# A gated linear attention and a rational feed-forward on one Trainium2 core: v loaded in fp32 and cast on chip into zero-padded heads

## The chip, the cores and the metric

The kernel runs on one core of one Trainium2 chip. The metric is the device time of one execution in microseconds (us). Three timed runs of the kernel before gave 215.76, 216.56 and 216.99 us; the median is 216.56 us.

## What is computed

Two stages follow one another. The first is a linear attention with a gate per key channel, for 4 batches and 8 heads over 768 time steps with heads 48 wide:

```python
f = 1.0 / (1.0 + np.exp(-f_logit))
for t in range(S):
    state = f[:, :, t, :, None] * state + np.einsum('bhd,bhe->bhde', k[:, :, t], v[:, :, t])
    y[:, :, t] = np.einsum('bhd,bhde->bhe', q[:, :, t], state)
```

The 8 heads of y are laid side by side to x, 3072 rows of 384. The second stage multiplies x by `w_in` (384 x 2048), puts every element through a rational function and multiplies by `w_out` (2048 x 384):

```python
h = x @ w_in
P = a[0] + a[1]*h + a[2]*h**2 + a[3]*h**3
Q = 1.0 + abs(b[0])*abs(h) + abs(b[1])*h**2
out = (P / (Q + 1e-06)) @ w_out
```

## The kernel before

The work is cut into 12 units of 256 time steps of one batch: unit n holds batch n mod 4 and stretch n div 4 of the time axis. Within a unit, two blocks of 128 steps are computed in chunked form. Partitions hold pairs of time steps, so a loaded tile of q, k, v or the gate has the form partition, head, i (the step of the pair), channel.

**The order of the work** is written out by hand in a table, `ORDER` (lines 19 to 98). Each entry is the name of a step with a unit number, sometimes a range of head pairs or column blocks, a PSUM slot (`@2`) and a mark (`>ls.1`: begin behind that step). The table is run from first to last, and each engine and each DMA queue takes its instructions in that order; between engines semaphores see to the dependencies. The steps that matter here:

- `ld n f|k|q` (line 193) loads the gate logits, keys or queries of a unit in fp32 on SP's queue. `ld n v` loads v on POOL's (GpSimd's) queue, and that DMA casts it from fp32 to bf16 on the way.
- `ef`, `ls` (lines 271, 276) on ScalarE (ACT) make the logarithm of the gate, `cs` (286) sums it along time on TensorE (PE), `A` (302) takes exponentials on ACT, `xa` (308) multiplies q or k by them on VectorE (DVE), `T` and `Te` (320, 330/332) transpose the results.
- `sc` (345) forms the scores of a block on PE, and `mk` (353) multiplies them by the causal mask while it moves them from PSUM to SBUF, on DVE.
- `kv` (414) multiplies keys by v into the new state on PE, `ae` (441) and `st` (445) apply the decay. `yi` and `yb` (367) form y: `yi` from the old state, `yb` from the masked scores and v. `ye` (435/436) moves y out.
- `yb` writes y transposed, in pieces of 32 channels. Two heads have 96 channels and so three pieces; the middle one takes the last 16 channels of the even head and the first 16 of the odd one. For it, v has to lie as 32 columns with zeros in the other half: `vm n 0` and `vm n 1` (line 360) copy the 16 columns of the even and of the odd heads into a tile `vmp` whose middle 16 columns were set to zero once (line 235). These copies run on POOL.
- `wi` and `wo` (199, 205) load `w_in` and `w_out` in four parts each, on POOL's queue, with a cast to bf16. `h` (454) and `ha`, `hb` (478) are the products with `w_in`; `hy`, `ab`, `sq`, `p1`, `p2`, `pm`, `ln`, `lz`, `ex`, `gm` are the steps of the rational function on DVE and ACT; `zd` and `ta` (519, 549) add two tiles with an accumulating DMA on POOL's queue; `o` (567) is the product with `w_out`, `so` (580) the store.

A loaded tile has three buffers (line 139), also v's. `vmp`, the padded q and k and the states are allocated once, in two copies that units use in turn.

In the table, v's load for unit 0 stands first on POOL's queue, then `vm 0 1`, then the first part of `w_in` (`wi 8 12`), then the second (`wi 12 16 >ls.1`), which begins behind unit 1's logarithm.

## Time and profile before

| what | value |
|---|---|
| median of the timed runs | 216.56 us (215.76 to 216.99) |
| span of the profiled execution, first to last instruction | 214.4 us |
| median of the runs less that span | 2.2 us |
| instructions | 7128 |
| granted TensorE clock, mean | 1.000 |
| POOL busy | 83.7 us |
| moved by DMA | 43.20 MB, of these 25.17 MB read from HBM |
| DMA packets under 512 bytes | 51184 of 61199 |

The profile was taken of one execution. Its own time lies around the span: what precedes the first instruction and follows the last one isn't in the span, and the median of the timed runs is 2.2 us above it. Rows of the timeline give the start, the duration, the engine, the line, the operation, what is written and read, and in square brackets the idle time of the engine just before and what ended it. POOL's time as a queue (its DMA instructions) and as an engine (its copies) stand in the same rows. A DMA row of the issues gives the time from issue to landing.

### The profile page before, as it was taken

The numbers are of one execution on the slowest core, as the hardware profiler recorded it, in microseconds if no ns is written. First come the engines' busy times: TensorE is split into PE (matmuls) and PEld (weight loads), VectorE is DVE, ScalarE is ACT, GpSimd is POOL, SyncE is SP. The second block draws the span as 40 slices with busy tenths as digits, with TensorE's granted clock in tenths as the row PEclk, the third lists the DMA queues.
The fourth block names the chain that finished last, engine by engine and source line by source line (L and its number), as shares of the span: only waits on it lengthen the run. The fifth ranks groups of instructions, "written<-read, shape, count | busy, mean of one in ns | idle before, by whom it ended". The sixth has DMA issues, their size and how long they took to land.

```text
span 214.4 us, 7128 instructions
## 1 busy us (share of the span) xinstructions
PE 201.0 (94%) x3166; PEld 139.9 (65%) x3166; DVE 201.7 (94%) x213; ACT 195.8 (91%) x204; POOL 83.7 (39%) x93
## 2 busy tenths in 40 slices
...
GB/s 143 240 257 217 201 242 197 195 223 223 187 200 248 247 235 219 253 228 203 192 292 193 81 294 215 209 225 208 89 192 200 164 196 126 174 282 151 187 84 148
DMA packets 61199, 43.20 MB, mean 202 GB/s; under 512 B 51184, under 2 KB 55024, under 8 KB 61168
## 3 DMA queue, kind: packets, MB, share of 16 engines
...
q8 instruction: 25, 0.41, 0.8%
q10 hardware_dynamic: 288, 0.20, 0.3%
...
HBM read 25.17 MB, written 4.72 MB: 139 GB/s over the span
## 4 chain that ended last, share of the span: by engine, by line
PE 39%; DVE 29%; ACT 14%; DMA 9%; issue 6%; SPq 2%; POOL 1%; DVEq 0%
PE hp L454 13%; PE op L567 12%; DVE gall L557 6%; DMA w_in_sb<-in_moe_w_in_dram 6%; DVE gall L545 4%; ACT qi L527 4%; ACT hy L484 4%; DVE z L497 3%; DVE h L489 3%; DVE scm L353 3%; DMA fn<-in_f_logit_dram 3%; PE u L505 3%; DVE gall L531 3%; PE y L367 2%; DVE hy L536 2%
## 5 line engine op out<-in xcount | busy, mean ns | idle before, releaser
L567 PE MATMUL op<-w_out_sb,gall 128*128 128x384 bf16 x384 | 69.2, 326 | 0.4 <-DVE gall L557 0.4
L454 PE MATMUL hp<-xT,w_in_sb 128*128 128x256 bf16 x564 | 66.7, 273 | 2.1 <-DMA w_in_sb<-in_moe_w_in_dram 2.0
L454 PEld LDWEIGHTS <-w_in_sb 128*128 128x128 bf16 x564 | 54.2, 98 | 11.5 <-DMA w_in_sb<-in_moe_w_in_dram 2.5
L567 PEld LDWEIGHTS <-gall 128*128 128x128 bf16 x384 | 36.1, 98 | 23.6 <-DVE gall L557 0.8
L484 ACT CAST hy<-hp 128x1024 bf16<-128x1024 f32 x47 | 48.1, 1076 | 2.3 <-PE hp L478 1.4
L527 ACT ACTIVATE qi<-lq 128x2048 bf16<-128x2048 f32 (+1 forms) x26 | 48.0, 1861 | 0.1
L360 POOL COPY vmp<-vn 128x128 bf16<-128x128 bf16 x24 | 35.2, 1516 | 28.4 <-DMA vn<-in_v_dram 22.7
L549 POOL DMA_DIRECT2D gall<-hy x20 | 20.0, 1068 | 53.9 <-ACT lsp L276 10.6
L523 ACT ACTIVATE lq<-z 128x2048 f32<-128x2048 bf16 (+1 forms) x20 | 36.8, 1874 | 0.0
L353 DVE TENSOR_TENSOR scm<-sc,mask 128x1024 bf16<-128x1024 f32 x24 | 29.0, 1215 | 1.9 <-PE sc L345 1.7
L489 DVE TENSOR_TENSOR h<-hy 128x4096 bf16<-128x4096 bf16 (+2 forms) x19 | 28.5, 1500 | 0.0
L557 DVE TENSOR_TENSOR gall<-gall,qi 128x4096 bf16<-128x4096 bf16 (+2 forms) x17 | 28.2, 1666 | 0.2
L545 DVE TENSOR_TENSOR gall<-gall,h 128x4096 bf16<-128x4096 bf16 (+2 forms) x17 | 28.1, 1652 | 0.0
L519 POOL DMA_DIRECT2D z<-h x17 | 19.3, 1366 | 17.0 <-PE u L505 6.0
L302 ACT ACTIVATE A<-cs 128x768 f32<-128x768 f32 (+1 forms) x26 | 19.4, 799 | 1.8 <-PE cs L286 1.8
L193 POOL DMA_DIRECT2D vn<-in_v_dram x12 | 12.4, 1030 | 15.7 <-PE y L367 7.9
L531 DVE TENSOR_SCALAR gall<-hy,a_sb 128x4096 bf16<-128x4096 bf16 (+1 forms) x14 | 16.9, 1208 | 0.0
L536 DVE TENSOR_SCALAR hy<-hy,a_sb 128x4096 bf16<-128x4096 bf16 (+1 forms) x14 | 16.6, 1185 | 0.0
L497 DVE TENSOR_SCALAR z<-hy 128x4096 uint16<-128x4096 uint16 (+2 forms) x19 | 15.7, 834 | 0.4 <-ACT hy L484 0.4
L330 ACT COPY qkT<-tp 128x1024 f32<-128x1024 f32 x11 | 11.6, 1058 | 3.2 <-PE tp L320 3.2
L320 PE MATMUL tp<-ident,qkp 128*128 128x128 bf16 x192 | 12.9, 219 | 0.8 <-DVE qkp L308 0.5
L320 PEld LDWEIGHTS <-qkp 128*128 128x128 bf16 x192 | 11.5, 98 | 2.5 <-DVE qkp L308 0.9
...
## 6 DMA issues: line engine op xcount, KB each, us to landing
...
fn<-in_f_logit_dram SPq DMA_DIRECT2D x11, 384.0 KB, 8.5
kn<-in_k_dram SPq DMA_DIRECT2D x11, 384.0 KB, 12.1
qn<-in_q_dram SPq DMA_DIRECT2D x11, 384.0 KB, 11.3
out_dram<-osb SPq DMA_DIRECT2D x11, 384.0 KB, 5.1
...
w_in_sb<-in_moe_w_in_dram POOLq DMA_DIRECT2D x4, 384.0 KB, 10.1
```

Source lines behind the costliest of these rows:

```text
L320: nc.tensor.transpose(t[:, x, i, p, :], s["qk"][:, i, x, 2 * p:2 * p + 2, :].rearrange("t h d -> t (h d)"), ident)
L353: return nc.vector.tensor_mul(t, s["sc", g].rearrange("s r a i t -> s (r a) (i t)"), mb)
L360: nc.gpsimd.tensor_copy(s["vm"][:, :, :, 32 * x:32 * x + 16], src)
L454: nc.tensor.matmul(t[:, m - m0, :], w_in_sb[:, kk, m * P:(m + 1) * P], s["x"][:, kk].rearrange("p i j t -> p (i j t)"), start=(kk == 0), s ...
L484: (nc.scalar.copy if eng == "s" else nc.vector.tensor_copy)(fl(big(s, "hy", "hy", 3), m0, m1), fl(s["hp", m0], 0, m1 - m0))
L489: return nc.vector.tensor_mul(fl(big(s, "h2", "h2", 2), m0, m1), fl(s["hy"], m0, m1), fl(s["hy"], m0, m1))
L523: nc.scalar.activation(fl(lq, m0, m1), fl(s["z"], m0, m1), AF.Ln, scale=regs[2], bias=1.0 + 1e-6)
L527: nc.scalar.activation(fl(qi, m0, m1), fl(lq, m0, m1), AF.Exp, scale=-1.0)
L531: return nc.vector.tensor_scalar(fl(big(s, "g", "gall", 3), m0, m1), fl(s["hy"], m0, m1), a_sb[:, 3:4], a_sb[:, 2:3], op0=ALU.mult, op1=AL ...
L545: return nc.vector.tensor_mul(fl(s["g"], m0, m1), fl(s["g"], m0, m1), fl(s["h2"], m0, m1))
L557: return nc.vector.tensor_mul(fl(s["g"], m0, m1), fl(s["g"], m0, m1), fl(qi, m0, m1))
L567: nc.tensor.matmul(s["op", j][:, j, 0:DM], s["g"][:, m, P * j:P * j + P], w_out_sb[:, m, :], start=(s["on", j] == 1), stop=(s["on", j] == KF))
```

## The change

v is now loaded like q and k: in fp32, on SP's queue, into a tile `vn` with one buffer. A new step `vc n par` (line 360 again) casts the four even heads (`par` 0) or the four odd heads (`par` 1) to bf16 into a new tile `vpd`, which has for each head 64 columns: an even head in columns 0 to 47, an odd head in columns 16 to 63, the other 16 set to zero once. So the three pieces of 32 columns of a head pair can be read from `vpd` as they stand; `vm`, `vmp` and the reads of `vn` by `yb` and `kv` are gone. The casts run on POOL, except those of unit 0: `vc 0 0 s` runs on ACT and `vc 0 1 v` on DVE. Each unit's load of v stands right behind the second cast of the unit before. Eighteen of the 22 casts on POOL have a mark (`>pm.2.0.16`) that holds them until a DVE step is done; in most cases the step that follows on DVE is an `mk`. The mask is stored in bf16.

```diff
-    mask = consts.tile([P, 2, 2, R], F32, name="mask")
+    mask = consts.tile([P, 2, 2, R], BF16, name="mask")
-    vmp = [consts.tile([P, 2, HP, 48], BF16, name=f"vmp{i}") for i in range(2)]
+    vpd = [consts.tile([P, HP, 2, 2, E], BF16, name=f"vpd{i}") for i in range(2)]
 def load(n, what, *args):
-        eng = nc.gpsimd if what == "v" else nc.sync
-            s[what] = ld.tile([P, H, 2, D], BF16 if what == "v" else F32, name=what + "n")
+            s[what] = ld.tile([P, H, 2, D], F32, name=what + "n", bufs=1 if what == "v" else 3)
-        i = eng.dma_start(...)
+        i = nc.sync.dma_start(...)
 def const_z(i):
-            nc.vector.memset(vmp[i][:, :, :, 16:32], 0.0)
+            nc.vector.memset(vpd[i][:, :, 0, :, D:E], 0.0)
+            nc.vector.memset(vpd[i][:, :, 1, :, 0:E - D], 0.0)
-    def vm(n, x):
-        s = unit(n)
-        vv = s["v"].rearrange("p (a r) i d -> p r i a d", r=2)
-        src = vv[:, 0, :, :, 32:48] if x == 0 else vv[:, 1, :, :, 0:16]
-        nc.gpsimd.tensor_copy(s["vm"][:, :, :, 32 * x:32 * x + 16], src)
+    def vc(n, par, *args):
+        s = unit(n)
+        hold = [x[1:] for x in args if x.startswith(">")]
+        copy = nc.scalar.copy if "s" in args else (nc.vector if "v" in args else nc.gpsimd).tensor_copy
+        i = copy(s["vp"][:, :, par, :, 16 * par:16 * par + D],
+                 s["v"].rearrange("p (a r) i d -> p r a i d", r=2)[:, par])
+        if hold:
+            behind(i, hold[0])
+        return i
 def yb(n, a0=0, a1=HP, sl=None):
-                        if kk == 1:
-                            w = s["vm"][r, i0, a, 16 * par:16 * par + 32]
-                        else:
-                            w = s["v"][r, 2 * a + par, i0, 16 * par:16 * par + 32]
+                        e = 32 * (kk - par)
+                        w = s["vp"][r, a, par, i0, e:e + 32]
 def kv(n, sl=None):
-                                         s["qk"][r, i, 1, 2 * a + par, :], s["v"][r, 2 * a + par, i, :],
+                                         s["qk"][r, i, 1, 2 * a + par, :], s["vp"][r, a, par, i, 16 * par:16 * par + D],
 ORDER, two places
-ld 0 q 0 2; ld 1 f; ld 0 v; ab_ a s; ...
-xa 0 1 0 2; T 0 2 4 @0; vm 0 1; kv 0 @3; Te 0 2 4; wi 8 12; ...
+ld 0 q 0 2; ld 0 v; ld 1 f; ab_ a s; ...
+xa 0 1 0 2; T 0 2 4 @0; vc 0 0 s; vc 0 1 v; ld 1 v; kv 0 @3; Te 0 2 4; wi 8 12; ...
```

The order on the engines at three places follows, the kernel before first and the change second. On POOL at the start of the program, behind the constants, before (`vn_158`, `vn_355` and `vn_445` are v of units 0, 1 and 2):

```order
L193 DMA vn_158<-in_v_dram 128x8x96
L360 COPY vmp0_94<-vn_158 128x8x16 [waits DMASW0_49]
L199 DMA w_in_sb_110<-in_moe_w_in_dram 128x3x512
L199 DMA w_in_sb_110<-in_moe_w_in_dram 128x3x512 [waits Activation_49]
L360 COPY vmp0_94<-vn_158 128x8x16
L193 DMA vn_355<-in_v_dram 128x8x96
L199 DMA w_in_sb_110<-in_moe_w_in_dram 128x3x512 x2
L193 DMA vn_445<-in_v_dram 128x8x96
```

And with the change (`vn_220`, `vn_541`, `vn_846` are v of units 1, 2 and 3):

```order
L199 DMA w_in_sb_110<-in_moe_w_in_dram 128x3x512
L199 DMA w_in_sb_110<-in_moe_w_in_dram 128x3x512 [waits Activation_49]
L199 DMA w_in_sb_110<-in_moe_w_in_dram 128x3x512 x2
L360 CAST vpd1_95<-vn_220 128x4x2x48 [waits DMAHW4_49,DVE_49]
L360 CAST vpd1_95<-vn_220 128x4x2x48 [waits DVE_49]
L550 DMA gall_673<-hy_467 128x2048 [waits DVE_49,Activation_49]
L205 DMA w_out_sb_111<-in_moe_w_out_dram 128x4x384
L360 CAST vpd0_94<-vn_541 128x4x2x48 [waits DMAHW5_49,PE_49]
L360 CAST vpd0_94<-vn_541 128x4x2x48 [waits PE_49]
L360 CAST vpd1_95<-vn_846 128x4x2x48 [waits DVE_49,DMAHW2_49,PE_49,Pool_49]
L360 CAST vpd1_95<-vn_846 128x4x2x48 [waits DVE_49,Pool_49]
```

The first part of `w_in` moved from behind v's load and the first copy to the first place on POOL's queue, and it waits for nothing. The change is described as issuing this part behind unit 0's logarithm; in the table it stands behind that step, but as the rows show no wait ties it to ACT. The second part still waits for ACT (unit 1's logarithm).

On SP's queue around units 2 to 5, before (`fn_535`, `qn_581`, `kn_755`, `kn_758` and `fn_762` are f 4, q 4, k 5, k 4 and f 6):

```order
L193 DMA fn_535<-in_f_logit_dram 128x8x96 [waits DMAHW3_49,DMAHW2_49,Activation_49]
L193 DMA qn_581<-in_q_dram 128x8x96 [waits DVE_49]
L193 DMA kn_755<-in_k_dram 128x8x96 [waits DMAHW4_49]
L193 DMA kn_758<-in_k_dram 128x8x96 [waits DMAHW5_49,DVE_49]
L193 DMA fn_762<-in_f_logit_dram 128x8x96 [waits DMAHW6_49,Activation_49]
L193 DMA fn_1110<-in_f_logit_dram 128x8x96 [waits DMAHW7_49,DMAHW2_49,Activation_49]
```

And with the change (`vn_541`, `vn_846`, `vn_952` and `vn_1193` are v of units 2, 3, 4 and 5):

```order
L193 DMA fn_536<-in_f_logit_dram 128x8x96 [waits DMAHW5_49,DMAHW4_49,Activation_49]
L193 DMA vn_541<-in_v_dram 128x8x96 [waits Pool_49]
L193 DMA qn_584<-in_q_dram 128x8x96 [waits DMAHW6_49,DVE_49]
L193 DMA kn_757<-in_k_dram 128x8x96 [waits DMAHW7_49]
L193 DMA kn_760<-in_k_dram 128x8x96 [waits DMAHW0_49,DVE_49]
L193 DMA fn_764<-in_f_logit_dram 128x8x96 [waits DMAHW1_49,Activation_49]
L193 DMA vn_846<-in_v_dram 128x8x96 [waits DMAHW5_49,DMAHW2_49,Pool_49]
L193 DMA vn_952<-in_v_dram 128x8x96 [waits DMAHW3_49,DMAHW2_49,Pool_49]
L193 DMA fn_1114<-in_f_logit_dram 128x8x96 [waits DMAHW4_49,Activation_49]
L193 DMA vn_1193<-in_v_dram 128x8x96 [waits DMAHW3_49,Pool_49]
```

The loads of v have come into this queue, each with a wait for a cast on POOL, and unit 3's now stands behind q 4, k 5, k 4 and f 6.

On DVE at unit 0, before (the first three rows multiply q and k by the exponentials; `qkT` is `Te`, `scm` is `mk`):

```order
L308 TENSOR_TENSOR qkp0_87<-qn_135,A_89 128x2x4x48 [waits DMAHW5_49,Activation_49]
L308 TENSOR_TENSOR qkp0_87<-kn_127,A_89 128x2x4x48 [waits DMAHW4_49,Activation_49]
L308 TENSOR_TENSOR qkp0_87<-kn_127,A_89 128x2x4x48 [waits DMAHW3_49,Activation_49]
L332 COPY qkT_258<-tp_207 128x4x256 [waits PE_49]
L308 TENSOR_TENSOR qkp0_87<-qn_135,A_89 128x2x4x48 [waits DMAHW6_49,Activation_49]
L353 TENSOR_TENSOR scm1_282<-sc_264,mask_85 128x1024 [waits PE_49]
```

And with the change:

```order
L309 TENSOR_TENSOR qkp0_87<-qn_136,A_89 128x2x4x48 [waits DMAHW5_49,Activation_49]
L309 TENSOR_TENSOR qkp0_87<-kn_128,A_89 128x2x4x48 [waits DMAHW4_49,Activation_49]
L309 TENSOR_TENSOR qkp0_87<-kn_128,A_89 128x2x4x48 [waits DMAHW3_49,Activation_49]
L360 CAST vpd0_94<-vn_157 128x4x2x48 [waits DMAHW7_49]
L333 COPY qkT_263<-tp_209 128x4x256 [waits PE_49]
L309 TENSOR_TENSOR qkp0_87<-qn_136,A_89 128x2x4x48 [waits DMAHW6_49,Activation_49]
L354 TENSOR_TENSOR scm1_287<-sc_269,mask_85 128x1024 [waits PE_49]
```

A cast that waits for v's load has come in front of `Te` and of everything that DVE does after it.

159 lines of the change are left out of this document (80 added, 79 removed).

## The prediction

> **What bounds the kernel now.** I read the page's shares of the span first, then the busy times by stretches of the span, to see whether one engine leads.
>
> ```profile
> PE 201.0 (94%) x3166; PEld 139.9 (65%) x3166; DVE 201.7 (94%) x213; ACT 195.8 (91%) x204; POOL 83.7 (39%) x93
> ```
> The stretches:
> ```profile
> 40.00:60.00 20.00, 19.39 (x352) 13.55 (x352) 20.00 (x22) 19.89 (x23) 5.89 (x10) 1.00 1.20 209
> 60.00:100.00 40.00, 40.00 (x653) 28.45 (x651) 40.00 (x34) 40.00 (x45) 19.02 (x16) 1.00 1.17 232
> ```
>
> The columns behind the stretch and its length are busy us of PE, PEld, DVE, ACT and POOL, then clock, DMA share and GB/s. From 60 to 100 us PE, DVE and ACT are all busy without a gap. So after the start nothing can be gained by an earlier transfer, and whatever makes any of the three wait comes out at the end nearly in full. POOL is 39% busy: the copies that go from it are worth nothing by themselves. What counts is (1) how late or early the three engines leave the start, (2) new waits behind v's load and casts, (3) what POOL's work costs DVE.
>
> The start, in the timeline. PE's waits and DVE's:
>
> ```profile
> 16.81 1.48 PE L454 MATMUL hp<-xT,w_in_sb 128*128 128x256 bf16 x12 [1.74 <-DMA w_in_sb<-in_moe_w_in_dram]
> 18.13 1.06 PE L320 MATMUL tp<-ident,qkp 128*128 128x128 bf16 x16
> 21.08 0.61 PE L478 MATMUL hp<-xT,w_in_sb 128*128 128x256 bf16 x4 [1.90 <-DMA w_in_sb<-in_moe_w_in_dram]
> 24.13 0.44 PE L414 MATMUL sv<-vn,qkp 64*64 64x48 bf16 x32 [0.23 <-DMA vn<-in_v_dram]
> ```
> DVE in the same stretch, and a little later:
> ```profile
> 9.44 0.69 DVE L332 COPY qkT<-tp 128x1024 bf16<-128x1024 bf16 x1 [0.24 <-PE tp L320]
> 10.04 0.55 DVE L308 TENSOR_TENSOR qkp<-qn,A 128x384 bf16<-128x384 f32 x1
> ...
> 17.00 0.73 DVE L259 TENSOR_SCALAR a_sb<-a_sb,sig 128x3 f32<-128x3 f32 x3
> 18.33 1.23 DVE L484 CAST hy<-hp 128x1024 bf16<-128x1024 f32 x1 [0.60 <-PE hp L454]
> ...
> 19.93 0.42 DVE L497 TENSOR_SCALAR z<-hy 128x1024 uint16<-128x1024 uint16 x1
> ...
> 22.09 1.23 DVE L353 TENSOR_TENSOR scm<-sc,mask 128x1024 bf16<-128x1024 f32 x1 [1.74 <-PE sc L345]
> 23.24 0.68 DVE L489 TENSOR_TENSOR h<-hy 128x1024 bf16<-128x1024 bf16 x1
> ...
> 25.29 0.56 DVE L445 TENSOR_TENSOR state<-sv,alast 128x384 bf16<-128x384 f32 x1 [0.23 <-ACT alast L441]
> ```
> ```profile
> 31.98 0.69 DVE L497 TENSOR_SCALAR z<-hy 128x2048 uint16<-128x2048 uint16 x1 [0.35 <-ACT hy L484]
> ```
>
> PE waits for `w_in` twice, 1.74 and 1.90 us, and DVE's waits behind that (0.60, 1.74, 0.23, 0.35) add to 2.92 us. That is all an earlier `w_in` could give.
>
> **The change part by part.** I count shifts against the profiled execution, whose span is 214.4 us; the median of the timed runs is 216.56, so 2.2 us lie around the span, and I carry them unchanged.
>
> *Unit 0's v.* When the loads land is seen where an engine stops waiting for them:
>
> ```profile
> 4.38 0.52 ACT L271 ACTIVATE fn<-fn 128x384 f32<-128x384 f32 x1 [2.29 <-DMA fn<-in_f_logit_dram]
> 5.10 0.52 ACT L271 ACTIVATE fn<-fn 128x384 f32<-128x384 f32 x1 [0.20 <-DMA fn<-in_f_logit_dram]
> 5.66 0.94 ACT L276 ACTIVATE lsp<-fn 128x384 bf16<-128x384 f32 x2
> ...
> 10.79 0.84 ACT L271 ACTIVATE fn<-fn 128x768 f32<-128x768 f32 x1 [0.37 <-DMA fn<-in_f_logit_dram]
> 11.70 0.84 ACT L276 ACTIVATE lsp<-fn 128x768 bf16<-128x768 f32 x1
> ...
> 15.38 0.60 ACT L436 ACTIVATE xT<-y 128x512 bf16<-128x512 f32 x1
> ```
> POOL's queue in the same stretch:
> ```profile
> 3.11 1.06 POOL L193 DMA_DIRECT2D vn<-in_v_dram  x1
> 9.40 0.28 POOL L360 COPY vmp<-vn 128x128 bf16<-128x128 bf16 x1 [5.23 <-DMA vn<-in_v_dram]
> 9.63 0.76 POOL L199 DMA_DIRECT2D w_in_sb<-in_moe_w_in_dram  x1
> 12.83 0.77 POOL L199 DMA_DIRECT2D w_in_sb<-in_moe_w_in_dram  x1 [2.44 <-ACT lsp L276]
> ...
> 14.72 1.50 POOL L199 DMA_DIRECT2D w_in_sb<-in_moe_w_in_dram  x2
> ```
>
> v 0 now has the place on SP's queue that f 1 had, and f 1 landed at 10.8; the same bytes follow one another there. On POOL's queue the first part of `w_in` takes the place of v's cast (issue to landing 7.1 us from 9.63 to 16.8, against 6.2 us from 3.11 to 9.4), so the competition in that stretch is about the same. I take 10.8 for v 0; 9.4 (the old time) and 12.2 (one load of 1.44 us later; the halves of f 0 land 0.72 us apart) are the ends. Then DVE's cast: the nearest row is 128x384 from fp32 in 0.55 us (line 308); I take 0.45, ends 0.2 and 0.55. `Te` starts at 10.8 + 0.45 instead of 9.44: DVE and with it unit 0 are **1.8 us later**. The cast on ACT (about 0.5 us, as the f 0 rows) lies beside it in ACT's wait for f 1. The extra memset and the bf16 mask cost nothing: they lie in DVE's waits before 7.7 us, and `mk` reads PSUM as before at 1.23 us for 1024 columns, with ends of nothing either way.
>
> *Unit 0 onward.* `ye` ended at 15.98 and h's first product could have started then, but waited for `w_in` until 16.81. Now that part is there, and the product starts at 17.8: 1.0 late. DVE's coefficients ended at 17.73, so `hy` now starts at 19.5 instead of 18.33, 1.2 late, and `ab` ends at 21.6.
>
> *The second part of `w_in`* waits for unit 1's logarithm (11.70 + 0.84). f 1 lands one load later, 12.2, so its issue is at 14.2 instead of 12.83. Before, it landed 8.2 us after issue with the first part still ahead of it; with nothing ahead I take the 6.2 to 7.1 us of the two transfers above: 20.4 to 21.3. PE is there at 20.3 (the transposes, `T`, ended at 19.2, and follow h's product, 1.0 later), so it resumes at 20.9, 0.2 earlier than 21.08, and `mk` of unit 1 starts near 22.0 as before. **The shift is back to about 0** there: PE's two waits have paid for v's delay. If the transfer takes 8.2 again, it is 1.3.
>
> *Unit 1's casts.* `kv 1` now waits for two POOL casts, the second held behind `sq` (23.24 to 23.92). What a cast takes:
>
> ```profile
> 0.31 0.10 POOL L610 MEMSET const-float32-0.0<- 128x1 f32 x1 [0.31 <-issue]
> ```
> The copies of before (shortest, median, longest), and one that was held up:
> ```profile
> L360 POOL COPY vmp<-vn x24: 283/662/5924, 9.4 to 156.4; 128x128 bf16<-128x128 bf16 x24
> ```
> ```profile
> 60.74 4.63 POOL L360 COPY vmp<-vn 128x128 bf16<-128x128 bf16 x1 [2.45 <-DMA vn<-in_v_dram]
> ```
>
> Undisturbed, 128 columns took 0.283 us and one column 0.10; the line through them gives 0.65 us for 384 columns (ends 0.4 and 0.85, three copies). So `kv 1` starts at 23.92 + 0.15 + 0.65 = 24.7 instead of 24.13, and `st` at 25.9: **+0.6**. The later parts of `w_in` are issued at 15 to 16 us as before, but with one part and two v casts fewer ahead of them; the 0.35 at 31.98 goes: **-0.3**. Start in all: **+0.3 us** (ends -1.4 and +2.0).
>
> *Unit 2.* v 2 is issued behind unit 1's second cast (24.7) and behind f 5 and f 4 on the queue. I take 36 for its landing, between 34.4 (the issue and the 9.7 us that a load of v took at that stretch, below) and the 38.3 at which `kv 2` stood. PE has 0.99 us to spare just behind that:
>
> ```profile
> 40.51 0.24 PE L367 MATMUL y<-scm,vn 64*32 64x128 bf16 x4 [0.99 <-DVE scm L353]
> ```
>
> I cost it at nothing; that cover is gone if v 2 lands after 38, and then each us is paid.
>
> *Unit 3* is the place that decides. Before, v 3 and v 4 were issued together and had a queue of their own:
>
> ```profile
> 33.91 1.75 POOL L193 DMA_DIRECT2D vn<-in_v_dram  x2
> ```
> Their two landings, from the accesses to `vn` in that stretch, and what PE and DVE did with unit 3:
> ```profile
> DMA to landing us min/median/max: 8.0/8.9/9.7
> ```
> ```profile
> 44.85 0.44 PE L414 MATMUL sv<-vn,qkp 64*64 64x48 bf16 x32
> ```
> ```profile
> 50.66 0.64 PE L345 MATMUL sc<-qkT 48*64 48x128 bf16 x32
> ```
> ```profile
> 51.13 1.23 DVE L353 TENSOR_TENSOR scm<-sc,mask 128x1024 bf16<-128x1024 f32 x1
> ```
>
> The second was issued at 34.8 and landed 9.7 us later, at 44.5, just before `kv 3` at 44.85. Now `vn` has one buffer: v 3 can't be issued before both casts of unit 2 (about 38), stands on SP's queue behind q 4, k 5, k 4 and f 6, and its own two casts come before `kv 3`. How that queue moves there:
>
> ```profile
> 37.14 5.66 SPq L193 DMA_DIRECT2D fn<-in_f_logit_dram  x1
> ```
> Its landing:
> ```profile
> fn<-in_f_logit_dram SPq DMA_DIRECT2D x1, 384.0 KB, 14.8
> ```
> The packets of the two kinds of queue, from the DMA view:
> ```profile
> q0 software_dynamic: 501, 0.41, 84.5%
> q1 hardware_dynamic: 496, 0.19, 36.2%
> ```
>
> The first two rows are f 6, issued at 37.1 and landed 14.8 us later at 51.9; the others are the packets from 21 to 24 us: while both queues have work, they go one for one, so SP's small packets (384 B) are held up by POOL's large ones. Lower end for v 3: five loads of 1.44 us behind 36 give 43.2. Upper end: behind f 6 at the old pace, 51.9 + 1.44 = 53.3. The v casts have left the other queue, but `ta 0` and `wo 8 12`, which stood behind them, move forward into this stretch. I take 45.3, nearer to the lower end, since two v casts less stand against one fp32 load more in this stretch. Two casts of 0.65 and a wait of 0.5 for the port: `kv 3` at 47.1 instead of 44.85 + 0.3. **+2.0 us.** Nothing hides it: the scores of unit 3 (50.66) follow on PE, and `mk` (51.13) starts on DVE in the moment they come, with no idle time before it.
>
> *The rest.* From unit 5 on a load of v has about a unit's time (214.4 / 12, some 18 us) between the cast that releases it and the next cast: nothing. Copies on POOL lengthen DVE's steps by about 0.1 us where they meet; they go, while some casts that are late meet DVE instead of `mk`: 0 for both together, ends -1.0 and +3.
>
> On that port the Trainium skill has a rule: "SBUF — State Buffer", section "Who interferes with whom", says that GpSimd and a DVE step with two SBUF inputs or in a 2-port mode exclude each other for a whole instruction, and that a DVE step with one SBUF input doesn't. The copy at 60.74, held for 4.63 us under such steps, agrees; by the rule a cast under `mk`, which reads PSUM and the mask, is free, and one of 0.65 us elsewhere could cost DVE up to that.
>
> Sum: 0.3 + 0 + 2.0 + 0 = **+2.3 us**, span 216.7, time 216.56 + 2.3 = **218.9 us**.
>
> **The rivals.**
> - *Faster: `w_in` early wins, and v 3 is in time.* For it: PE's 1.74 + 1.90 us. Against it: v 0 behind q on SP's queue. If v 0 lands at 9.9, unit 0 is 0.9 late, `mk` of unit 1 can start at 21.0 (-1.1), `kv 1` costs 0.3 and 31.98 gives 0.35 back: -1.2; with v 3 landed by 43.3 nothing is added, and 0.2 less meeting of copies gives -1.4: 215.2 us. It decides whether v 3 lands before 43.5.
> - *No difference:* the start gains about as much as `kv 3` costs (-1.2 and +1.2): 216.6 us.
> - *SP's queue gets stuck.* Each v load waits for a POOL cast, and f, q and k wait behind it. If v 3 lands at 50 or casts off `mk` cost DVE 0.5 each ten times: +5 to +6, 222 us. At 53.3 it would be about +10.
> - *The change doesn't do what it says:* the first part of `w_in` isn't held behind unit 0's logarithm (that ended at 5.66 + 0.94 = 6.6). That is settled by the order; held, q 0 and v 0 would have the transfers to themselves for some 3 us more, and unit 0 would be up to 1 us earlier. It has no chance of its own.
>
> "DMA: Bandwidth & Descriptors" of the Trainium skill, section "Queues, rings and completion order", has each DMA engine go round the queues a whole packet at a time. The 501 and 496 packets agree. By it the first part of `w_in`, at 3.11 us, would hold up q 0 with its large packets more than v's cast did; with q 0 later by 1 us the sum would be 219.9.
>
> **How the numbers follow.** Forecast 0.50 (217.7 to 220.7), faster 0.18 (215.2), no difference 0.17, stuck queue 0.15 (221 to 226). The range leaves out about 0.08 below and 0.08 above: 215.2 to 222.5 us. A measurement of this kernel can tell about 0.5% (1.1 us) from no change: faster 0.18, same 0.17, slower 0.65.
>
> **What would show it.** `Te` of unit 0 near 11.3 behind a cast on DVE that waited for v; PE at h's first product without a wait for `w_in`; `mk` of unit 1 near 22; a wait of PE at `kv 3` of 1 to 3 us, ended by POOL's cast, and behind it gaps on DVE and ACT near 48 to 54 that weren't there. If `kv 3` doesn't wait, the forecast is wrong toward the faster side; if `ha` waits for the second part of `w_in` past 22.4, or q 5 and k 6 come late behind v 5 (PE, DVE and ACT with holes from 60 to 100), toward the slower.

## The result, and the profile after

The changed kernel takes 235.41 us (median of 4 runs, 234.42 to 236.21), the kernel before on the same chip 216.78 us (215.76 to 217.53): a ratio of 1.086, interval 1.082 to 1.091, or 18.6 us slower. The forecast was 218.9 us, 2.3 us slower, with a range up to 222.5: the direction was right and the size wrong by a factor of eight. The profiled execution took 236.21 us, of these 234.5 in its span, at a mean granted clock of 0.956 (before: 214.4 and 1.000). Where single executions of one kernel lie far apart (e2, e10 and e13 below), they are given one by one.

One thing has to be known to read this time rightly. The changed table has the casts of units 10 and 11 ahead of `yb 8` and `yb 9` and in the same two tiles, so in units 8 and 9 `yb` multiplies the scores by v of units 10 and 11 (in e2 to e4, e7 to e9, e11 and e12 too). The amount of work is the same, but v 10 is needed at `yb 8` already, not at `kv 10`.

The page of the changed kernel: the shares of the span, the granted clock in 40 slices, the second line of the chain that ended last, and one of the costliest groups.

```profile
PE 207.7 (89%) x3158; PEld 143.9 (61%) x3166; DVE 202.0 (86%) x216; ACT 197.0 (84%) x205; POOL 58.5 (25%) x79
...
PEclk9979999995999999999999999559999999999999
...
PE op L568 11%; PE hp L455 10%; DMA vn<-in_v_dram 8%; DVE gall L558 6%; DVE h L490 6%; DVE gall L546 5%; DVE scm L354 4%; DMA gall<-hy 4%; DVE z L498 4%; DVE qkp L309 4%; DVE gall L532 3%; SPq L193 3%; PE tp L321 3%; DVE hy L537 3%; PE y L370 3%
...
L360 POOL CAST vpd<-vn 128x384 bf16<-128x384 f32 x22 | 15.5, 720 | 61.9 <-DMA vn<-in_v_dram 26.4
```

DVE is as busy as before (202.0 us against 201.7): the work hasn't grown, the holes have. The chain now has loads of v with 8% of 234.5 us, 19 us; before, no load of v stood among its lines. The clock has two holes, in slice 10 and in slices 26 and 27, each where PE had waited for POOL's cast, and a third, shorter one in slice 3 (0.57 from 14 to 16 us and 0.58 to 18), where PE had waited for unit 0's cast on ACT. To place the loss I follow `mk` through the units. On DVE, after (units 1, 2, 3, 8 and 9):

```profile
25.44 1.23 DVE L354 TENSOR_TENSOR scm<-sc,mask 128x1024 bf16<-128x1024 f32 x1 [0.83 <-PE sc L346]
...
42.68 1.21 DVE L354 TENSOR_TENSOR scm<-sc,mask 128x1024 bf16<-128x1024 f32 x1
...
61.43 2.36 DVE L354 TENSOR_TENSOR scm<-sc,mask 128x1024 bf16<-128x1024 f32 x2 [0.41 <-PE sc L346]
...
140.03 2.34 DVE L354 TENSOR_TENSOR scm<-sc,mask 128x1024 bf16<-128x1024 f32 x2
164.53 1.23 DVE L354 TENSOR_TENSOR scm<-sc,mask 128x1024 bf16<-128x1024 f32 x1 [1.02 <-PE sc L346]
```

Before, they started at 22.09, 39.24, 51.13, 129.73 and 144.78 (units 1 and 3 are shown in the prediction, units 2, 8 and 9 here):

```profile
39.24 1.21 DVE L353 TENSOR_TENSOR scm<-sc,mask 128x1024 bf16<-128x1024 f32 x1
...
129.73 2.34 DVE L353 TENSOR_TENSOR scm<-sc,mask 128x1024 bf16<-128x1024 f32 x2
...
144.78 1.21 DVE L353 TENSOR_TENSOR scm<-sc,mask 128x1024 bf16<-128x1024 f32 x1
```

The shift is 3.35, 3.44, 10.30, 10.30 and 19.75 us; the span of this execution is 20.1 us longer. So there are three steps and next to nothing between them: **the start +3.4, unit 3 +6.9, units 8 to 10 +9.4**.

The start, in the timeline of the changed kernel:

```profile
8.70 0.56 DVE L309 TENSOR_TENSOR qkp<-qn,A 128x384 bf16<-128x384 f32 x1 [1.62 <-DMA qn<-in_q_dram]
12.50 0.36 DVE L360 CAST vpd<-vn 128x384 bf16<-128x384 f32 x1 [2.30 <-DMA vn<-in_v_dram]
12.77 0.69 DVE L333 COPY qkT<-tp 128x1024 bf16<-128x1024 bf16 x1
```

PE's wait for unit 0's cast, and its products with `w_in`, a little later:

```profile
13.06 0.44 PE L415 MATMUL sv<-vpd,qkp 64*64 64x48 bf16 x32 [2.66 <-ACT vpd L360]
...
20.98 1.47 PE L455 MATMUL hp<-xT,w_in_sb 128*128 128x256 bf16 x12 [0.96 <-ACT xT L437]
24.44 0.60 PE L479 MATMUL hp<-xT,w_in_sb 128*128 128x256 bf16 x4 [1.10 <-ACT qkT L331]
```

In this execution PE no longer waits for `w_in`. But q 0 and v 0 come late: DVE starts on q at 8.70 us, and `Te`, which started at 9.44, starts at 12.77 behind the cast of v. The second `mk` of unit 0 stands at 17.95 instead of 13.00, 4.95 us later and not 3.3, since PE runs at the lower clock in between.

Unit 3, on SP's queue (start and the time until the queue takes the next one; the last row is v 3 and v 4), in the DMA view for v 3, and on PE:

```profile
34.23 1.24 SPq L193 DMA_DIRECT2D qn<-in_q_dram  x1
35.52 5.28 SPq L193 DMA_DIRECT2D kn<-in_k_dram  x2
40.89 3.16 SPq L193 DMA_DIRECT2D fn<-in_f_logit_dram  x1
44.16 8.39 SPq L193 DMA_DIRECT2D vn<-in_v_dram  x2
```
```profile
vn<-in_v_dram SPq DMA_DIRECT2D x1, 384.0 KB, 6.4
```
```profile
51.76 0.18 PE L415 MATMUL sv<-vpd,qkp 64*64 64x48 bf16 x1 [3.39 <-POOL vpd L360]
53.00 1.87 PE L321 MATMUL tp<-ident,qkp 128*128 128x128 bf16 x16
54.98 2.77 PE L455 MATMUL hp<-xT,w_in_sb 128*128 128x256 bf16 x12
```

v 2 landed at 38.46; then q 4, k 5, k 4, f 6 and v 3, which was issued at 44.16 and landed at 50.58: 12.1 us for five loads, 2.4 us each. PE waits 3.39 us at `kv 3`, and behind the wait the transposes and the products with `w_in` (16 and 12 matmuls) take 1.87 and 2.77 us; as many took 1.06 and 1.48 us before. `kv 3` starts 6.91 us later than before and `mk 3` 10.30: of the 6.9 us that unit 3 adds, 3.5 are the wait and 3.4 what follows it at the lower clock.

Units 8 to 10, on SP's queue, POOL and PE:

```profile
136.63 1.38 SPq L193 DMA_DIRECT2D kn<-in_k_dram  x1
138.06 3.76 SPq L193 DMA_DIRECT2D qn<-in_q_dram  x1
141.92 11.65 SPq L193 DMA_DIRECT2D vn<-in_v_dram  x2
```
```profile
134.80 1.72 POOL L520 DMA_DIRECT2D z<-h  x2 [2.85 <-issue]
152.21 0.96 POOL L360 CAST vpd<-vn 128x384 bf16<-128x384 f32 x2 [14.05 <-DMA vn<-in_v_dram]
```
```profile
152.78 1.50 PE L370 MATMUL y<-scm,vpd 64*32 64x128 bf16 x64 [7.80 <-POOL vpd L360]
```

v 10 was issued at 141.92, behind three stores, k 11 and q 10, beside the two large accumulating transfers `zd 6` that POOL had issued from 134.80. It landed at 152.06; both casts followed in 0.96 us, and PE, which stood at `yb 8`, had waited 7.80 us. The stretches around the two waits (busy PE, PEld, DVE, ACT and POOL, then the clock):

```profile
50.00:55.00 5.00, 2.97 (x58) 2.67 (x58) 1.34 (x2) 1.00 (x3) 3.01 (x4) 0.68 0.28 58
55.00:60.00 5.00, 4.72 (x23) 2.93 (x23) 2.37 (x4) 3.52 (x4) 0.00 (x0) 0.63 1.17 220
...
150.00:155.00 5.00, 2.17 (x67) 1.41 (x68) 0.00 (x0) 0.00 (x0) 2.61 (x4) 0.50 0.20 32
155.00:160.00 5.00, 5.00 (x35) 2.99 (x33) 3.00 (x4) 3.43 (x5) 0.00 (x0) 0.74 1.05 222
```

From 155 to 160 us PE is busy without a gap and yet gets only 0.74 of its clock: the wait is paid a second time. The Trainium skill, "TensorE: Matmul & The Clock Gate", section "HAM oscillation — how this bites in real kernels", says that PE must not stand idle for more than about 3.4 us, or it goes on at half its clock; the wait of 7.80 us agrees and the one of 3.39 lies at that figure. The start doesn't: there the waits were 1.05 and 2.66 us, with 0.62 us of work between them, and the clock still stood at 0.50 from 15 to 17 us. So in this case a shorter wait was enough.

### The profile page after: what moved, and what is told of

It is laid out like the page before. It is cut to its first block, busy times and chain, and to the rows that moved or that the text cites. A ratio compares the mean times of both kernels' runs of the same rounds, so it can differ in the third digit from the quotient of the medians.

```text
span 234.5 us, 7147 instructions
## 1 busy us (share of the span) xinstructions
PE 207.7 (89%) x3158; PEld 143.9 (61%) x3166; DVE 202.0 (86%) x216; ACT 197.0 (84%) x205; POOL 58.5 (25%) x79
## 4 chain that ended last, share of the span: by engine, by line
DVE 38%; PE 37%; DMA 12%; issue 6%; SPq 3%; ACT 1%; POOL 1%; DVEq 0%; POOLq 0%
PE op L568 11%; PE hp L455 10%; DMA vn<-in_v_dram 8%; DVE gall L558 6%; DVE h L490 6%; DVE gall L546 5%; DVE scm L354 4%; DMA gall<-hy 4%; DVE z L498 4%; DVE qkp L309 4%; DVE gall L532 3%; SPq L193 3%; PE tp L321 3%; DVE hy L537 3%; PE y L370 3%
## 5 line engine op out<-in xcount | busy, mean ns | idle before, releaser
L568 PE MATMUL op<-w_out_sb,gall 128*128 128x384 bf16 x384 | 70.3, 330 | 0.4 <-DVE gall L558 0.4
L455 PE MATMUL hp<-xT,w_in_sb 128*128 128x256 bf16 x564 | 68.2, 276 | 1.0 <-ACT xT L437 1.0
L455 PEld LDWEIGHTS <-w_in_sb 128*128 128x128 bf16 x564 | 55.0, 99 | 11.0 <-issue 1.7
L568 PEld LDWEIGHTS <-gall 128*128 128x128 bf16 x384 | 36.6, 99 | 24.5 <-issue 1.3
L360 POOL CAST vpd<-vn 128x384 bf16<-128x384 f32 x22 | 15.5, 720 | 61.9 <-DMA vn<-in_v_dram 26.4
L520 POOL DMA_DIRECT2D z<-h x17 | 18.4, 1152 | 48.1 <-DVE h L490 18.3
L550 POOL DMA_DIRECT2D gall<-hy x20 | 20.1, 1086 | 40.4 <-ACT alast L442 7.6
L370 PE MATMUL y<-scm,vpd 64*32 64x128 bf16 x768 | 11.8, 226 | 9.0 <-POOL vpd L360 7.8
L309 DVE TENSOR_TENSOR qkp<-kn,A 128x768 bf16<-128x768 f32 (+1 forms) x13 | 11.8, 915 | 8.1 <-ACT A L303 8.1
L446 DVE TENSOR_TENSOR state<-sv,alast 128x384 bf16<-128x384 f32 x20 | 11.0, 552 | 6.9 <-PE sv L426 6.3
L370 PEld LDWEIGHTS <-vpd 64*32 64x32 bf16 x768 | 8.5, 93 | 13.0 <-POOL vpd L360 8.3
```

What stands on the lines that cost most here:

```text
L370: nc.tensor.matmul(s["y"][32 * qd:32 * qd + 32, j, blk * C:blk * C + C].rearrange("e (i t) -> e i t", i=2), lhsT, rhs, start=(j, qd) not i ...
L455: nc.tensor.matmul(t[:, m - m0, :], w_in_sb[:, kk, m * P:(m + 1) * P], s["x"][:, kk].rearrange("p i j t -> p (i j t)"), start=(kk == 0), s ...
L568: nc.tensor.matmul(s["op", j][:, j, 0:DM], s["g"][:, m, P * j:P * j + P], w_out_sb[:, m, :], start=(s["on", j] == 1), stop=(s["on", j] == KF))
```

## The experiments

The theory (A in the expectations) was that loads of v, now in SP's queue and with one buffer, are late in three places, and that each place can be mended by itself. The rivals (B) were, case by case, that the loss moves on to the next load, or that it comes from something else: the casts, the tile with zeros, the clock. Where a diff names steps, it is of the table.

### Unit 8: the casts behind `yb`

`e1_cast_behind_yb8` gives `yb` of units 8 and 9 its own v again (these two units are computed as in the kernel before):

```diff
-... mk 8 0; vc 10 0 >xa.9.0; ... mk 8 1; vc 10 1 >mk.8.0; ld 11 v; ls 11; ... yb 8 0 2; cs 10 @0
+... mk 8 0; ... mk 8 1; ls 11; ... yb 8 0 2; vc 10 0 >xa.9.0; vc 10 1 >mk.8.0; ld 11 v; cs 10 @0
 (and vc 11 0, vc 11 1 likewise, behind yb 9 0 2)
```

> The changed kernel with the casts of units 10 and 11 (and the load of v 11 between them) moved in the table to behind yb 8 and yb 9, which read the same tiles. v 10 stays where it was on SP's queue and lands late, near 152 us. Theory A (yb 8 waits for unit 10's cast only because the table puts that cast ahead of it into the same tile): PE's wait of 7.8 us at yb 8 goes, with it DVE's of 8.1 and ACT's of 8.4, kv 10 finds its v in time, and the time falls by 8.5 to 10 us, to 225.5 to 227. Rival B (SP's queue is the limit there, and whoever needs v 10 or v 11 next pays): the wait moves to kv 10 or kv 11 and the time falls by less than 3 us.

229.12 us (228.54 to 231.67), ratio 1.058 (1.047 to 1.069): 6.3 us less than the changed kernel, between A and B. POOL's row of this run shows what was left:

```profile
151.25 3.66 POOL L359 CAST vpd<-vn 128x384 bf16<-128x384 f32 x2 [13.97 <-DMA vn<-in_v_dram]
156.63 2.10 POOL L519 DMA_DIRECT2D z<-h  x2
```

PE's wait at `yb 8` is gone, but v 10 lands as late as ever (151.10), and POOL's queue stands 13.97 us in front of its cast. Behind the cast stands `zd 7`, so ACT waits 2.91 us for `z` at 167.77. So a late cast on the engine that also issues DMAs held back the DMAs behind it.

### Unit 3: v 3 ahead of q 4

`e2_v3_ahead_of_q4`:

```diff
-... ld 2 v; kv 1 @3; ld 4 q; ...   ... sc 2 0 @0; vc 2 0; vc 2 1; ld 3 v; kv 2 @1; ...
+... ld 2 v; vc 2 0; vc 2 1; ld 3 v; kv 1 @3; ld 4 q; ...   ... sc 2 0 @0; kv 2 @1; ...
```

> The changed kernel with unit 2's casts and v 3's load moved in the table to right behind v 2's load, so ahead of q 4, k 5, k 4 and f 6 on SP's queue and ahead of ta 0 and a part of w_out on POOL's; vn keeps its one buffer. The computation is that of the changed kernel: units 8 and 9 still use the v of units 10 and 11 in yb. Theory A (the place on SP's queue makes v 3 late): v 3 is issued near 40.7 instead of 44.2, lands near 46 instead of 50.6, PE's wait of 3.4 us at kv 3 is nearly gone, and the time falls by 4 to 6.5 us, to 229 to 231.5. Rival B (the one buffer and the transfers against POOL's queue make it late): it lands past 49 and the time falls by less than 2 us.

229.57 us in the profiled execution and 229.79 in another; two more took 241.5 and 243.2, and of these there is no profile. The profiled one is 5.8 us under the changed kernel, as A had it. v 3 was issued at 39.18 and landed at 43.01. PE's row at `kv 3` and DVE's at `mk 3`:

```profile
47.69 0.44 PE L414 MATMUL sv<-vpd,qkp 64*64 64x48 bf16 x32
```
```profile
53.96 2.36 DVE L353 TENSOR_TENSOR scm<-sc,mask 128x1024 bf16<-128x1024 f32 x2
```

No wait at `kv 3`, and `mk 3` at 53.96 instead of 61.43: the second step is gone when v 3 doesn't stand behind q 4, k 5, k 4 and f 6. The same move puts `ta 0` and `wo 8 12` behind unit 2's casts on POOL's queue (issued at 39.10 and 39.71 instead of 34.17 and 34.78), and this run doesn't take the two apart.

### The clock by itself

`e4_warm_in_the_waits` adds matmuls whose results nobody reads, so that PE is busy in the two waits:

```diff
+... yb 2 2 4; dz 12 @3; kv 3 @3; ...
+... pm 6 0 16; dz 28 @3; yi 8 1 @3; ...
```

> The changed kernel with products that nobody reads put ahead of kv 3 (12 of 128x512) and of yi 8 and yb 8 (28), where PE otherwise sits and waits for 3.4 and 7.8 us; the waits themselves stay. The computation is that of the changed kernel: units 8 and 9 still use the v of units 10 and 11 in yb. Theory A (behind each wait PE's granted clock is about one half for some us, which costs on top of the wait): the granted clock from 50 to 60 and from 145 to 160 us rises from 0.5 to 0.75 to near 1, the mean clock from 0.96 to over 0.98, and the time falls by 2.5 to 4.5 us, to 231 to 233. Rival B (a wait costs what it lasts, DVE and ACT are behind anyway): no change, within 0.8 us of 235.4.

230.86 us (230.17 to 231.63), 4.5 us less; A held, with its time 0.1 us below the range. The stretches behind the two waits, in this run:

```profile
50.00:55.00 5.00, 3.98 (x74) 3.12 (x73) 2.29 (x3) 2.42 (x4) 2.98 (x4) 1.00 0.36 78
...
150.00:155.00 5.00, 5.00 (x66) 3.57 (x51) 2.70 (x3) 3.99 (x6) 1.10 (x2) 1.00 0.87 180
```

The loads were still late; only the clock stayed at 1.00 there. From the cast of v 3 to `mk 3` it is now 7.72 us and not 10.70, from that of v 10 to `mk 9` 10.30 and not 12.32: 5.0 us together. So of the 18.6 us some 4.5 are paid behind these two waits, not in them. The start's lower clock isn't in this number.

### The start: `w_in` held

`e3_w_in_held` makes the first part of `w_in` really wait for unit 0's logarithm; `e8_held_f2_first` also puts `ld 2 f` ahead of `ld 1 v`; `e12_start_alone` also holds the third and fourth part.

```diff
-wi 8 12
+wi 8 12 >ls.0.2.4                                  (e3, e8, e12)
-vc 0 1 v; ld 1 v; ...            ld 2 f >mk.0.1
+vc 0 1 v; ld 2 f; ld 1 v; ...                      (e8, e12)
-wi 4 8; ... xa 1 1; wi 0 4; ... xa 1 0; fb
+... xa 1 1; ... xa 1 0; wi 4 8 >xa.1.0; wi 0 4; fb    (e12)
```

> The changed kernel with the first part of w_in held behind unit 0's logarithm, as the change was described. The computation is that of the changed kernel: units 8 and 9 still use the v of units 10 and 11 in yb. Theory A (the first part of w_in at 3.1 us holds up q 0 and with it v 0, f 1 and all of the start): q 0 lands near 7.3 and 9, v 0 near 10.5 instead of 12.5, the start is 1.5 to 3 us shorter, and the time falls by as much, to 232.4 to 234. Rival B (the same bytes go through the same engines, so what q 0 gains f 1 and the second part of w_in lose): mk of unit 1 stays within 0.5 us of 25.4 and the time within 0.7 us.

> The changed kernel with the first part of w_in held behind unit 0's logarithm, and f 2 loaded ahead of v 1 and without its mark. The computation is that of the changed kernel: units 8 and 9 still use the v of units 10 and 11 in yb. Holding w_in alone made the start 3.7 us shorter at mk of unit 1 and then gave it back with a wait of 5.1 us for f 2, which was issued 0.24 us behind the second part of w_in. Theory A (that order of the two issues is all): f 2 lands before 18, that wait goes, the start stays 2.5 to 3.7 us shorter, and the time is 231.5 to 233. Rival B (what is saved ahead is given back by the next load that comes behind w_in, f 3, k 2 or q 2): the time is 234.5 or more.

> The changed kernel with the start alone mended: the first part of w_in held behind unit 0's logarithm, f 2 ahead of v 1 without its mark, and the third and fourth parts of w_in held behind xa of unit 1. The computation is that of the changed kernel: units 8 and 9 still use the v of units 10 and 11 in yb. With the first two of these alone f 2 landed at 25.3 and the time was 236.5. Theory A (f 2 and v 1 crawl while w_in's parts are moved, so holding two parts back frees them): f 2 lands before 20, v 1 before 23, mk of unit 1 stays near 21.8, kv 1 waits less than 1 us, and the time falls by 3 to 4 us, to 231.4 to 232.5. Rival B (the held parts are then late for h): PE waits for w_in at the third or fourth part and the time is 234.5 or more.

They took 237.69, 236.54 and 233.98 us (ratios 1.095, 1.090 and 1.079, the last 1.077 to 1.082). In e3 the start is mended as A had it: q 0 lands at 7.35 and 8.09, v 0 at 9.58 instead of 12.47, and `mk 1` stands at 21.73, 3.7 us earlier. But the second part of `w_in` now goes out at 13.03, just ahead of f 2 (13.27), and that load takes 13.0 us. The DMA view, and PE:

```profile
fn<-in_f_logit_dram SPq DMA_DIRECT2D x1, 384.0 KB, 13.0
```
```profile
28.02 0.48 PE L287 MATMUL cs<-lsp,Ui 128*128 128x384 bf16 x1 [5.14 <-ACT lsp L277]
```

In e8 f 2 is issued 2.5 us earlier and lands only 0.9 us earlier (25.32): it isn't its place on SP's queue that counts but what POOL has under way. Both theories missed the time of e3; in e8 the rival held, and e12 came out between the two. In e12, with two parts fewer under way, f 2 lands at 18.49 and `mk 1` stands at 21.55. But POOL reaches `ta 0` and `wo 8 12` 3.9 us earlier (30.28), now ahead of v 2, which takes 11.0 us:

```profile
43.55 0.19 PE L415 MATMUL sv<-vpd,qkp 64*64 64x48 bf16 x1 [5.68 <-POOL vpd L360]
```

3.9 us won at the start, 1.4 left at the end. What one load gains, the next one that stands beside POOL's transfers loses.

### v 10 early, and what stands behind it

`e7_v10_early` issues v 10 behind `yb 7`; `e9_q10_ahead` also puts q 10 and k 11 far ahead; `e11_zd_held` leaves v alone and holds `zd 6` instead.

```diff
+yb 7 0 2; vc 9 0; vc 9 1; ld 10 v; ...     (e7, e9; gone from behind sc 8 0)
+ld 11 q; ld 10 q; ld 11 k; ...             (e9; gone from behind h 7 4 8)
+xa 9 0; zd 6 8 16 >xa.9.0; zd 6 0 8; ...   (e11; gone from behind st 8 0 and o 4 0 12 16)
```

> The changed kernel with only unit 9's casts and v 10's load moved in the table to right behind yb 7, ahead of the stores, k 11 and q 10 on SP's queue; unit 10's and 11's casts stay ahead of yb 8 and yb 9, so the computation is that of the changed kernel: units 8 and 9 still use the v of units 10 and 11 in yb. Theory A (what was left over when only the casts were moved, 229.1 us and not 226, is POOL's queue standing behind a cast that waits for v 10, with zd 7 behind it): v 10 lands before 143, POOL never waits 14 us, zd 7 is issued before 155, and the time falls by 9 to 10.5 us, to 225 to 226.5. Rival B (the rest lies elsewhere): the time falls by 6 to 7 us as there.

> The changed kernel with unit 9's casts and v 10's load right behind yb 7 (as in the run that came out at 238.6 us with a wait for q 10), and now also q 10 and k 11 moved on SP's queue to right behind q 11, ahead of the three stores; units 10's and 11's casts stay ahead of yb 8 and yb 9, so the computation is that of the changed kernel: units 8 and 9 still use the v of units 10 and 11 in yb. Theory A (a load on SP's queue takes 1.4 us alone and 4 to 5 us while POOL's queue moves zd or ta, and whatever stands last there pays): q 10 lands before 135, v 10 before 143, nothing waits from 138 to 165, and the time falls by 9 to 10.5 us, to 225 to 226.5. Rival B (DMA as a whole is full there, so the next thing, v 11 or a zd, is late instead): 230 or more.

> The changed kernel with the two zd of unit 6 held behind xa of unit 9, about 5 us later, which is where they stood before the change in relation to DVE (there a copy of 5.9 us blocked POOL); nothing on SP's queue is moved, and casts stay where they are, so the computation is that of the changed kernel: units 8 and 9 still use the v of units 10 and 11 in yb. Theory A (v 10 is late because the two zd run beside k 11, q 10 and v 10 on SP's queue): v 10 lands near 144 instead of 152, the wait of 7.8 us at yb 8 falls to under 2, and the time falls by 6.5 to 9.5 us, to 226 to 229. Rival B (v 10 is late because it stands behind three stores and two loads, whatever POOL does): it lands after 149 and the time falls by less than 3 us.

e7 took 238.59 us (ratio 1.100), 3.2 us *more*, which neither theory had: v 10 lands at 140.30 and `yb 8` doesn't wait, but q 10, now behind it and the stores, takes 19.4 us, and DVE waits 11.96. The DMA view, and DVE:

```profile
qn<-in_q_dram SPq DMA_DIRECT2D x1, 384.0 KB, 19.4
```
```profile
159.73 0.96 DVE L309 TENSOR_TENSOR qkp<-qn,A 128x768 bf16<-128x768 f32 x1 [11.96 <-DMA qn<-in_q_dram]
```

e9 took 233.67, 233.79 and 235.53 us, and 1106 in a fourth execution, which is left out; B. `yb 8` is fine, and v 11 takes 20.9 us, so `yb 9` waits 6.47:

```profile
vn<-in_v_dram SPq DMA_DIRECT2D x1, 384.0 KB, 20.9
```

e11 took 234.04 us (ratio 1.079, 1.077 to 1.081). In it q 10, issued ahead of `zd 6`, takes 6.7 us instead of 12.8, but v 10, issued only 0.56 us ahead of that, still takes 11.0; `yb 8` waits 6.86. So `zd 6` beside the load is what makes it long, as A said of the mechanism, and the number was B's: v 10 landed at 150.36 us. Holding one transfer puts it on the next load.

### Mending several places at once

`e6_all_together` has e1, e3, e2's v 3, f 2 and v 2 moved forward, and e7. `e10_all_again` adds e9's and e12's moves. `e13_unit4_too` adds to e10 `ld 6 f` behind `ld 4 v` and `wo 12 16`, `wo 4 8`, `ta 1 8 16`, `wo 0 4` behind `vc 4 1`.

```diff
+vc 0 0 s; vc 0 1 v; ld 2 f; ld 1 v; ... wi 8 12 >ls.0.2.4
+vc 1 1 >sq.0.8.12; ld 2 v; ld 5 f; ld 4 f; vc 2 0; vc 2 1; ld 3 v; kv 1 @3; ld 4 q
+yb 7 0 2; vc 9 0; vc 9 1; ld 10 v; ...   yb 8 0 2; vc 10 0 >xa.9.0; vc 10 1 >mk.8.0; ld 11 v
```

> The changed kernel with v still in fp32 on SP's queue in one buffer, and the table mended at each place found so far: the first part of w_in held behind unit 0's logarithm, f 2 loaded ahead of v 1 and without its mark, v 2 ahead of f 5 and f 4, unit 2's casts and v 3 ahead of q 4, unit 9's casts and v 10 ahead of three stores, k 11 and q 10, and the casts of units 10 and 11 behind yb 8 and yb 9. Theory A (the places cost the time, not fp32 nor the one buffer): the three losses go together, no wait of PE over 1 us behind v after unit 0, and the time is 214 to 218. Rival B (one buffer and the fp32 bytes on SP's queue are too tight wherever they stand): a wait for v or for f, q, k remains somewhere and the time is 220 or more.

> The version with the whole table mended, with two places more: q 10 and k 11 ahead of the three stores, and the third and fourth parts of w_in held behind xa of unit 1, so that f 2 and v 1 land before them. Theory A (each loss is a load on SP's queue that runs while POOL's queue moves large packets; with the loads ahead, all go): no wait of PE over 1 us behind unit 0, and the time is 214 to 218. Rival B (the fp32 loads of v crowd SP's queue so that some other load is late): a new wait appears behind one of the moved transfers, and the time is 220 or more.

> The version with the whole table mended, which took 218.9 us in one execution and 231 to 234 in three where the load of v 4 landed past its place and its cast then took 6.2 us, with unit 4 mended as well: f 6 behind v 4 on SP's queue, and ta 1 and three parts of w_out behind unit 4's casts on POOL's. Theory A (fp32 and the one buffer cost nothing once every load of v runs clear of POOL's transfers): no wait of PE over 2 us behind v or its casts, and the time is 215.5 to 219 in all executions. Rival B (there is always a next place: an engine that runs earlier issues its zd or ta earlier, beside another load): a wait of 3 us or more appears elsewhere and the time is 221 or more.

e6: 236.04 us (ratio 1.087), B: v 1 lands at 26.30, and q 10 at 155.96. e10: 218.89 us in one execution, with a clock of 1.000 and without a profile, and 231.2, 231.75 and 234.04 in three others. In the profiled one (231.75, clock 0.982) v 4 comes past its place, and its cast meets DVE, which runs five instructions without a gap from 59.90 to 66.49 us:

```profile
60.78 6.16 POOL L358 CAST vpd<-vn 128x384 bf16<-128x384 f32 x1 [10.06 <-DMA vn<-in_v_dram]
```

e13: 224.5 to 232.4 us in six executions, median 228.2 (the three shortest against the kernel before: ratio 1.045, 1.038 to 1.051), B: in the profiled one (230.29) q 5, beside the parts of `w_out`, takes 20.3 us, and DVE waits 7.60 us for it.

With all known waits mended the kernel is still between 219 and 234 us, and it differs from one execution to the next. No single place in the table accounts for it.

### v on POOL's queue again

`e5_v_bf16_on_pool` keeps the casts and the padded heads, with e1's order, but loads v as before: in bf16 on POOL's queue, two buffers, start places as in the kernel before. `e14_bf16_held` adds the held `w_in` and e9's q 10 and k 11.

```diff
-s[what] = ld.tile([P, H, 2, D], F32, name=what + "n", bufs=1 if what == "v" else 3)
-i = nc.sync.dma_start(...)
+s[what] = ld.tile([P, H, 2, D], BF16 if what == "v" else F32, name=what + "n", bufs=2 if what == "v" else 3)
+i = (nc.gpsimd if what == "v" else nc.sync).dma_start(...)
```

> The changed kernel's padded heads and casts (now copies from bf16), but v loaded as before the change: by POOL's queue with a cast on the way, into two bf16 buffers, at the places that the loads of units 0 to 3 had before, later ones behind the copy that frees their buffer; unit 10's and 11's copies stand behind yb 8 and yb 9. Theory A (the loss lies in the way v comes in, on SP's queue and into one buffer, and the padded heads with 22 casts on POOL cost nothing that counts): the start is that of before within 1 us, no wait at kv 3 or yb 8, and the time is 215.5 to 219. Rival B (the 384-column casts on POOL hold up DVE or come late and cost by themselves): 222 or more, with DVE steps longer beside casts.

> The version with v in bf16 on POOL's queue into two buffers (224.6 us), with the first part of w_in held behind unit 0's logarithm, and q 10 and k 11 ahead of the three stores on SP's queue. Theory A (its 8 us over the kernel before were lost where POOL's copies had held back the first part of w_in and the zd of unit 6, not in padded heads or casts): the start is that of before within 1 us, no wait for q 10, and the time is 215.5 to 218.5. Rival B (the casts of 384 columns cost it): 221 or more.

224.63 us (ratio 1.036, 1.032 to 1.041) and 223.53 us (1.031, 1.026 to 1.036). Neither `kv 3` nor `yb 8` waits in e5; what is left is its start (+3.2 at `mk 2`), DVE's wait for q 10 (2.00 us) and ACT's for `z` (1.40 us at 177.71). The numbers were B's. e1, with the same order at `yb 8` and `yb 9`, took 229.12 us; so v on POOL's queue, in bf16, in two buffers and issued where it was before is worth 4.5 us more, all of these together, and some 7.5 us over the kernel before are left.

### The brake of before, and no loads at all

`e15_before_no_brake` is the *kernel before* with `vm 0 1` moved behind `wi 8 12`, so that the first part of `w_in` goes out early there too.

> The kernel before with one step moved: POOL's first copy (vm 0 1) stands behind the first part of w_in instead of ahead of it, so that this part is issued near 4.1 us and not at 9.6. Nothing of the computation changes. Theory A (that copy, waiting for v 0, was what kept w_in's large packets away from q 0, f 1 and k 1): q 0 and f 1 land 1 to 2 us later, mk of unit 1 starts 1.5 to 3.5 us later, and the time is 218 to 220. Rival B (an earlier w_in saves PE's wait of 1.7 us, and the loads go on as they were): the time is 215.5 to 217.

217.0 us against 216.45 (ratio 1.0016, 0.9985 to 1.0047): the same, B's number. The first part goes out at 4.15 instead of 9.63 us, q 0 lands later (9.60), and PE's wait for `w_in` goes in exchange: `mk 1` stands at 22.63, 0.5 us later. By itself the early `w_in` costs nothing that can be measured; with v 0 on SP's queue behind q 0 it does at `mk 1` (3.7 us against e3).

Last, the loads of v behind unit 0 are left out: all units cast unit 0's v. `e16_one_v_load` is the changed kernel with that alone, `e17_one_v_load_start` with e12's start as well.

```diff
 def load(n, what, *args):
+        if what == "v" and n > 0:
+            s["v"] = unit(0)["v"]
+            return
```

> The changed kernel without the loads of v behind unit 0's: all units cast and use unit 0's v, which is left in its buffer, so y is computed with the wrong v in 11 of 12 units. Casts, their marks, the padded heads and everything else stay. Theory A (behind the start, all of the loss is the loads of v on SP's queue and what waits for them): no wait at kv 3 or yb 8, the shift of 3.4 us at mk of unit 1 stays as it is to the end, and the time is 219 to 221. Rival B (the casts and the padded heads cost by themselves, on POOL's port or in POOL's queue): the shift grows on the way and the time is 222.5 or more.

> As the kernel with one load of v (y is computed with unit 0's v in 11 of 12 units), and with the start mended: the first part of w_in behind unit 0's logarithm, f 2 without its mark, the third and fourth parts of w_in behind xa of unit 1. Theory A (the start was lost to w_in's packets beside q 0, v 0 and f 1, and nothing else but v's loads costs): mk of unit 1 near 21.6, no wait for v 1 or f 2, and the time is 214.5 to 217. Rival B (the casts and padded heads cost by themselves): 219 or more.

220.80 us (220.44 to 220.92; ratio 1.019, 1.017 to 1.022), A; and 217.61 us (217.18 to 218.51; ratio 1.006, 1.003 to 1.009), between the two. The busy times of e17:

```profile
PE 201.8 (93%) x3158; PEld 140.3 (65%) x3166; DVE 202.5 (93%) x216; ACT 196.7 (91%) x205; POOL 55.6 (26%) x79
```

22 casts on POOL, two more elsewhere, the padded heads and the bf16 mask are all there, and PE's and DVE's shares are nearly those of the kernel before (94% each). So the loss splits: **235.41 - 220.80 = 14.6 us for the loads of v behind unit 0** (with what they push aside and the clock behind the waits), **220.80 - 217.61 = 3.2 us for the start**, and 217.61 - 216.68 (the kernel before beside it) = 0.9 us for everything else. None of the versions was faster than the kernel before.

## Why the prediction was right in direction and wrong in size

| step of the prediction | forecast | measured |
|---|---|---|
| `Te` of unit 0 starts | 11.25 (+1.8) | 12.77 (+3.3) |
| first product of `h` | 17.8 | 20.98 |
| `mk` of unit 1, second `w_in` part in time | near 22, shift 0 | 25.44, +3.35 |
| unit 2 | 0 (v 2 lands at 36) | +0.1 (38.46) |
| v 3 lands | 45.3 | 50.58 |
| unit 3 | +2.0 | +6.9 |
| from unit 5 on | 0 | 0 up to unit 8, then +9.4 |
| a cast on POOL, undisturbed | 0.65 | 0.51 |
| `mk` with a bf16 mask | as before, 1.23 | 1.22 |

**The start.** The step that failed is "the competition in that stretch is about the same". It put the first part of `w_in` in the place of v's cast load, 7.1 us against 6.2; but that part has 128x3x512 elements, v's load had 128x8x96, and so twice the bytes stand beside q 0, v 0 and f 1. q 0's halves landed at 8.60 and 11.07 instead of 7.27 and 9.24, and v 0 at 12.47, past the upper end of 12.2. e3 shows it: with `w_in` held v 0 lands at 9.58, and `mk 1` stands at 21.73. That PE's two waits for `w_in` would go was right of the first. The second was gone in this execution because PE came there late, with its clock at 0.57 from 14 to 18 us behind the wait for v 0's cast. In e2 and e4, whose table is the same up to there, the clock stayed at 1.00, PE did wait for the second part (2.25 and 1.93 us), and `mk 1` stood at 24.25 and 24.41, 2.2 and 2.3 us later than before. So the second part's landing, 20.4 to 21.3 in the prediction, was mis-sized too: 23.2 and 23.4 in these runs (issued at 15.14 and 15.51 instead of 14.2). The prediction's sentence by the Trainium skill, that `w_in` at 3.11 us would hold up q 0 by 1 us, came nearer than the sum that stood without it: 1.3 and 1.8 us. The remark that holding it would gain unit 0 up to 1 us was too small as well.

**Unit 3.** The mechanism was the one forecast, down to the wait of PE at `kv 3` ended by POOL's cast. The term that was mis-sized is the load on SP's queue: 1.44 us each, a figure from the start of the program. Five loads took 12.1 us, 2.4 each, and v 2 was 2.5 us later than assumed. 38.46 + 12.1 = 50.6, inside the stated 43.2 to 53.3, whose upper end I had and then didn't weigh: the row beside it, f 6's 14.8 us, was the better guide to a queue that has POOL's transfers beside it. This makes `kv 3` 3.5 us later; the other 3.4 us of unit 3 are the next point.

**What a wait costs.** The sum counted each wait once. PE's clock fell behind the waits of 2.66, 3.39 and 7.80 us, and e4 puts a price on the last two: 4.5 us. It was nowhere in the sum.

**The rest.** "From unit 5 on a load of v has about a unit's time (214.4 / 12, some 18 us) between the cast that releases it and the next cast: nothing" failed. It held up to unit 8, where the shift stays at +10.30. But the table has `vc 9 1`, which releases the buffer for `ld 10 v`, just ahead of `kv 9`, and `vc 10 0` six entries behind that load, ahead of `yb 8`: v 10 has next to no time. The order of the table, which I had, showed that; I read it around units 0 to 5 and carried the spacing on. e1 shows that it is so, and e7, e9 and e11 that mending it there alone only moves the wait, since `zd 6` and `zd 7` are beside whatever load comes next.

**The rivals.** The queue that gets stuck, with a chance of 0.15, was the one that came true; its price of 5 to 10 us comes near the start and unit 3 together (10.3 us) and leaves units 8 to 10 out. That it comes near is in part luck: for v 3 at 50 us it gave 5 to 6, and 3.4 of the 10.3 us are the start and 3.4 the lower clock, neither of which it had in that size. The faster rival needed v 3 before 43.5. No case had a second place with the same mechanism, and so the range ended at 222.5. The place that I named for more such waits, v 5 with q 5 and k 6 between 60 and 100 us, added nothing.

**What stays open.** In the kernel before, three copies on POOL took 6.40 us in front of `zd 6`:

```profile
121.45 6.40 POOL L360 COPY vmp<-vn 128x128 bf16<-128x128 bf16 x3 [0.49 <-issue]
127.78 1.64 POOL L193 DMA_DIRECT2D vn<-in_v_dram  x1
129.97 2.07 POOL L519 DMA_DIRECT2D z<-h  x2
```

k 11 and q 10 landed at 130.81 and 132.08 there, about when `zd 6` was issued. That slow copies kept POOL's large transfers out of the way of SP's loads is argued from this trace and fits e11; in unit 0 such a brake was worth nothing (e15). At units 8 to 10 it wasn't tried by itself. No run has v in fp32 on SP's queue with more than one buffer, so the share of the one buffer in the 14.6 us isn't known. Nor do the runs say why single executions of e2 and e10 lie 12 us apart.
